# Delta-rule attention and a gated feed-forward on one core: who makes the exponent words of the weights

## The chip, the core and the metric

The kernel runs on one NeuronCore of a Trainium2 chip. The core has a matrix engine (TensorE, PE in the profile, with its weight loads shown as PEld), a vector engine (VectorE, DVE), an activation engine (ScalarE, ACT), a general engine (GpSimd, POOL) and a queue engine that issues most of the transfers (SyncE, SP). Each engine takes its instructions strictly in the order in which they were written down for it and waits on semaphores for the others. The metric is the device time of one execution in microseconds (us).

## The reference, cut to what matters

Two blocks follow one another. The first is a delta-rule attention over 4 batches, 8 heads, 768 steps and 48 dimensions; the second is a feed-forward with 384 inputs, 2048 hidden units and a sigmoid-weighted activation.

```python
k_n = k / (norm(k) + 1e-6)
for t in range(S):                                    # attention, state 48 x 48 per head
    y[:, :, t] = q_t @ state
    state = state + beta_t * outer(k_t, v_t - state^T k_t)
x = y as (3072 tokens, 384)
h = x @ w_in                                          # 384 x 2048
out = (h / (1 + exp(-1.702 * h))) @ w_out             # 2048 x 384
```

`w_in` and `w_out` arrive in a 64-bit format (they are numpy products with a float64 scale; the kernel asserts that they are not fp32). [...] In the 64-bit word the upper 32 bits hold a sign, 11 bits of exponent and 20 bits of fraction; the lower 32 bits hold the rest of the fraction. The conversion makes a word whose exponent field is the 64-bit one less 896, clamped at zero ("the exponent word"), gives it the sign, builds the fraction as a number between 1 and 2, and multiplies the two.

## The kernel before, in words

The 768 steps are cut into 6 chunks of 128. A chunk of one batch is a unit, 24 units in all. In a unit the keys are normalized, turned, multiplied with themselves on TensorE (`gram`), and the diagonal blocks of 32 x 32 are inverted by VectorE in a long run of small multiplications and sums (`invert`, lines 543 to 628). With the inverses the unit's values are solved block by block (`solve`, `below`, `rest`): TensorE multiplies, ScalarE copies the result to `VU`, VectorE subtracts. Then come the outputs (`psY`, later `four`), copied by ScalarE to `xT`, the input of the feed-forward. `hidden` multiplies `w_in` with `xT` (`ph`), ScalarE evicts each pair of results through the activation to `gT` (or `TW`), and `both_written`, `written` and `seven` multiply `gT` with `w_out` (`po`). `ph` and `po` share two PSUM buffers (tag "moe").

The first 175 us are a prologue with its own order, written by hand. Every operation made through `vec`, `act`, `pe`, `pool` and `sync` is pinned to the program's order. In between stands background work, handed out by `fill(us)` (line 322): it pulls steps from the generator `background()` and subtracts the cost that each step yields until the budget is used up. The costs are the numbers in the `yield` lines, not measured times. The background is: the nine pieces of `w_in`, then the inversion of units 4 to 7 (`invert(1)`), then the fourteen pieces of `w_out`. A piece of `w_in` has 128 x 768 elements (two halves of each of the quarters 0, 1 and 3) or 128 x 512 (three thirds of quarter 2, called `thirds`, their words lying in `gT` buffers). A piece of `w_out` has 128 x 384 elements, two of them (named 4 and 6, each for two of the sixteen row blocks) 128 x 768. The order of `w_out` is 0, 1, 2, 3, 4 with 5, 6 with 7, 8, 13, 9, 10, 12, 11, 14, 15.

One piece (`conversion`, line 224) takes five VectorE operations and one on ScalarE, with `lo` and `hi` the lower and upper words at a stride of 8 bytes and `p` the destination seen as integers:

1. VectorE masks the exponent bits of `hi` into `p` ("the mask", cost 0.75).
2. ScalarE takes `p` times 8 plus `low`, clamped at zero ("low", cost 0).
3. VectorE joins the sign of `hi` to `p` ("the join", cost 0.95).
4. VectorE turns `hi` into 1.fraction as integers, in place (0.7).
5. VectorE adds the scaled `lo` (0.95).
6. VectorE multiplies with the destination (0.95).

`conversions` (line 275) is a pipeline of depth two: the mask and ScalarE's operation of the next piece are written down between steps 4 and 5 of this one, so a ScalarE result has two VectorE operations to arrive in. When a piece is done, `fetches` starts the transfer of a later one into the space that came free, on SP's queue.

Beside this, `prepare_early` (line 1366) prepares units 8 to 11 while the feed-forward of the first four units runs: `normalize_mixed` (line 348) squares the keys on ScalarE, sums them on VectorE (`ssq`), takes the power on GpSimd (`rn`), two small operations on VectorE, and scales the keys by eight small ScalarE operations (`KN`). TensorE's `turn` (`psT`) of that unit waits for these. It stands in TensorE's order between groups of `ph`. In the same way ScalarE's evictions of `ph` stand in ScalarE's order around the eight operations and around step 2 of the conversions.

Of the kernel before, what the change touches and what calls it, by code (L numbers as in the profile page):

```python
# [8 lines left out]
F32 = mybir.dt.float32  # L9
I32 = mybir.dt.int32  # L10
U32 = mybir.dt.uint32
AX = mybir.AxisListType
ALU = mybir.AluOpType
ACT = mybir.ActivationFunctionType
# [4 lines left out]
def kernel(  # L19
# [47 lines left out]
    cpool = ctx.enter_context(tc.tile_pool(name="const", bufs=1))  # L67
# [66 lines left out]
    vec, act, pe, pool = Engine(nc.vector), Engine(nc.scalar), Engine(nc.tensor), Engine(nc.gpsimd)  # L134
# [28 lines left out]

    low = cpool.tile([128, 1], F32, name="low")
    pool.memset(low, -896.0 * (1 << 23))
    raws = w_out.rearrange("p f d -> p (f d)").bitcast(I32)
    assert moe_w_in.dtype != F32 and moe_w_out.dtype == moe_w_in.dtype

# [38 lines left out]
    places, slots = {}, {}  # L207
# [13 lines left out]
        places[f] = as_raw(words, (1, DM))  # L221
        sync(out=as_rows(places[f])[:, 0], in_=moe_w_out[f * 128 : (f + 1) * 128, :])

    def conversion(dst, raw, shape):

        lo, hi = raw[:, :, :, 0], raw[:, :, :, 1]  # L230
        ts, stt = vec.tensor_scalar, vec.scalar_tensor_tensor
        AND, OR = ALU.bitwise_and, ALU.bitwise_or
        E1 = 1 << 20
        p = dst.bitcast(I32)
        ts(p, hi, 0x7FF * E1, None, op0=AND)
        yield 0.75
        act.activation(p, p, ACT.Relu, scale=8.0, bias=low)
        yield 0.0
        stt(out=p, in0=hi, scalar=-(1 << 31), in1=p, op0=AND, op1=OR)
        yield 0.95  # L240
        ts(hi, hi, E1 - 1, E1, op0=AND, op1=OR)
        yield 0.7
        f = lo.bitcast(F32)
        stt(out=f, in0=lo.bitcast(U32), scalar=2.0**-32, in1=hi, op0=ALU.mult, op1=ALU.add)
        yield 0.95
        stt(out=dst, in0=f, scalar=2.0**-20, in1=dst, op0=ALU.mult, op1=ALU.mult)
        yield 0.95

    def pieces():

        for i in range(4):
            if i == 2:
                for j in range(KC):
                    dst = w_in[:, j : j + 1, i * NQ : (i + 1) * NQ]
                    yield dst, thirds[j], (1, NQ), ("in", -j)
                continue
            for e in range(2):
                at = i * NQ + e * NPC
                raw = quarter(i)[:, :, e * NPC : (e + 1) * NPC, :]
                yield w_in[:, :, at : at + NPC], raw, (KC, NPC), ("in", 2 * i + e)  # L260
        i = 0
        while i < FC:
            f = order[i]
            if f in (4, 6):
                at = inside[f] * DM
                raw = as_raw(raws[:, at : at + 4 * DM], (2, DM))
                yield w_out[:, f : f + 2, :], raw, (2, DM), ("out", f)
                i += 2
            else:
                yield w_out[:, f : f + 1, :], None, (1, DM), ("out", f)  # L270
                i += 1
# [3 lines left out]
    def conversions():  # L275

        whole = list(pieces())

        def begin(i):
            dst, raw, shape, name = whole[i]  # L280
            ops = conversion(dst, places[name[1]] if raw is None else raw, shape)
            return ops, next(ops)

        after, cost = begin(0)
        next(after)
        yield cost
        for i in range(len(whole)):
            ops = after
            yield next(ops)
            yield next(ops)  # L290
            if i + 1 < len(whole):
                after, cost = begin(i + 1)
                yield cost
                next(after)
            yield next(ops)
            cost = next(ops)
            done.add(whole[i][3])
            fetches.pop(whole[i][3], lambda: None)()
            yield cost
# [11 lines left out]
    def background():  # L311

        converting = conversions()
        while ("in", 7) not in done:
            yield next(converting)
        yield from invert(1)
        done.add("inverse")
        yield from converting
# [13 lines left out]
    def normalize(n):  # L332
# [5 lines left out]
        ssq = wk.tile([128, H], F32, tag="ssq", name="ssq", bufs=4)  # L338
        vec.tensor_reduce(ssq, ksq, axis=AX.X, op=ALU.add)
        rn = wk.tile([128, H], F32, tag="rn", name="rn", bufs=4)  # L340
# [7 lines left out]
    def normalize_mixed(n):  # L348
# [4 lines left out]
        ssq = wk.tile([128, H], F32, tag="ssq", name="ssq", bufs=4)  # L353
        vec.tensor_reduce(ssq, ksq, axis=AX.X, op=ALU.add)
        rn = wk.tile([128, H], F32, tag="rn", name="rn", bufs=4)
# [8 lines left out]
    def normalize_first():  # L364
# [5 lines left out]
        for b in range(B):  # L370
            act.activation(sq[:, b % 2], KN[b][:, :, 0:D], ACT.Square)
            vec.tensor_reduce(s[:, b], sq[:, b % 2], axis=AX.X, op=add)
        roots(x, y, t, s)
# [4 lines left out]
    def roots(x, y, t, s):  # L378

        tt, ts, stt = vec.tensor_tensor, vec.tensor_scalar, vec.scalar_tensor_tensor  # L380
        mult, add = ALU.mult, ALU.add
        ts(x, s, 1e-30, None, op0=ALU.max)
        ts(y.bitcast(I32), x.bitcast(I32), -0.5, float(0x5F3759DF), op0=mult, op1=add)
        for k in range(3):
            if k == 2:
                warm(NR, vec.memset)
            stt(out=t, in0=y, scalar=-0.5, in1=y, op0=mult, op1=mult)
            tt(t, t, x, op=mult)
            stt(out=y, in0=t, scalar=1.5, in1=y, op0=add, op1=mult)
        tt(s, s, y, op=mult)  # L390
        ts(s, s, 1e-6, None, op0=add)
        vec.reciprocal(s, s)
# [10 lines left out]
    def roots_second(areas):  # L403

        z, r = (TW[:, a : a + B * H].rearrange("p (b h) -> p b h", b=B) for a in (1792, 1856))
        for o in range(2):
            vec.tensor_reduce(z[:, 2 * o : 2 * o + 2], areas[o], axis=AX.X, op=ALU.add)
        pool.tensor_tensor(r, z, half[:, 0:1].broadcast_to([128, B, H]), op=ALU.pow)
# [134 lines left out]
    def invert(c, b0=0, nb=B):  # L543
# [10 lines left out]
        def dots(o, a, b, ny, nx, nk, negate):  # L554

            P = wk.tile([128, ny, nx, nk], F32, tag="P", name="P", bufs=1)[part]
            tt(P, a, b, op=ALU.mult)
            red(o, P, axis=AX.X, op=ALU.add, negate=negate)

# [9 lines left out]
        def diag(t, off, dims):  # L569
            return bass.AP(t.tensor, t.offset + off, [t.ap[0], [step, 2]] + dims)  # L570

        for i in range(1, HS):
# [4 lines left out]
            )  # L577
            red(diag(Yf, i, [[BS, i]]), P, axis=AX.X, op=ALU.add, negate=True)
            yield 0.35 + i * i / 240
# [652 lines left out]
    for blk in range(NB):  # L1232
# [3 lines left out]
        out=YB, in_=YB, compare_op=ALU.not_equal, fill=1.0, base=0,  # L1236
# [37 lines left out]
    for at in range(B):  # L1274
        for u in range(2):
            for half_ in range(2):
                lane = at * BS + u * 2 + half_
                other_queue(
                    out=bL[lane : (at + 1) * BS : NB],
# [165 lines left out]
```

## Time and profile before

| what | value |
|---|---|
| median of 3 runs (lowest, highest) | 721.5 us (720.91, 723.11) |
| profiled execution: its time, its span | 722.29 us, 720.6 us |
| busy: PE, DVE, ACT, POOL | 675.7, 467.4, 232.3, 251.4 us |
| mean granted clock of TensorE | 0.973 |

The span is the time from the first to the last instruction of the profiled execution. Busy times are sums over the span; an engine that is busy most of the time in one stage can be idle in the next, so the stages are read one by one. In the lists of groups and of single instructions, `out<-in` are the program's names with buffer numbers left out; `128x384` is partitions by elements; nearly all operations show line 122, the line of the helper that records them, so they are told apart by names and shapes. A matrix product of fp32 operands leaves two records. A wait is written as "engine tile <- what released it: total us, times, longest us".

### The profile page before, as it was taken

To read this page: it belongs to the slowest core of one execution; us is meant where nothing else is said; L and a number is where in the kernel's file an instruction comes from. 1 tells how busy PE (TensorE), PEld (TensorE's weight loads), DVE (VectorE), ACT (ScalarE), POOL (GpSimd) and SP (SyncE) were. 2 spreads that over 40 slices of the span, in tenths; PEclk is the share of its full clock that TensorE was granted. 3 is DMA by queue.
4 is the path that set the end of the run, shared out by engine and by line. 5 is a ranking of instruction groups with operands and counts; after the bars stand their busy time and mean duration, and the time that the engine had idled before them with its cause. 6 is when DMAs were issued, how large, how long until landed. Compare 5 with 4: busy or idle time off the path is not lost.

```text
span 720.6 us, 20434 instructions
## 1 busy us (share of the span) xinstructions
PE 675.7 (94%) x8779; PEld 583.0 (81%) x8779; DVE 467.4 (65%) x880; ACT 232.3 (32%) x553; POOL 251.4 (35%) x258
## 2 busy tenths in 40 slices
PE   9288898996999999999999999999999999999997
PEld 7166767863668888998988988988988988989997
DVE  4899999798465398497597696795793892110000
ACT  3362533561233313313323333233323223122020
POOL 6084001240237641652642733622522403304032
PEclk9678999998999999999999999999999999999999
DMA  8895854631223213214114124213122111000100
GB/s 175 142 186 110 209 108 82 144 100 45 56 51 65 51 32 83 43 37 93 28 36 93 27 48 82 45 43 63 34 52 56 32 25 31 8 23 2 28 0 23
DMA packets 129179, 46.66 MB, mean 65 GB/s; under 512 B 118848, under 2 KB 123584, under 8 KB 129088
## 3 DMA queue, kind: packets, MB, share of 16 engines
q1 hardware_dynamic: 125664, 40.94, 27.7%
q0 software_dynamic: 2240, 4.02, 2.6%
q8 instruction: 69, 1.13, 0.7%
q10 hardware_dynamic: 1184, 0.39, 0.2%
q14 instruction: 22, 0.18, 0.1%
HBM read 33.13 MB, written 11.01 MB: 61 GB/s over the span
## 4 chain that ended last, share of the span: by engine, by line
PE 54%; DVE 32%; DMA 5%; issue 4%; ACT 3%; SPq 2%; DVEq 0%; POOL 0%; ACTq 0%; POOLq 0%
PE ph L122 25%; PE po L122 17%; DVE P L122 12%; DVE YB L122 6%; PE four L122 4%; DVE w_out L122 4%; DVE NT L122 3%; DVE VU L122 3%; DMA NT<-Nd 2%; PE psT L122 2%; PE ps_warm L122 2%; PE psU L122 2%; DMA Nd<-G 2%; PE psR L122 1%; DVE w_in L122 1%
## 5 line engine op out<-in xcount | busy, mean ns | idle before, releaser
L122 PE MATMUL ph<-xT,w_in 128*128 128x256 f32 x1152 | 259.6, 383 | 2.0 <-ACT gT L122 2.0
L122 PEld LDWEIGHTS ph<-xT,w_in 128*128 128x128 f32 x1152 | 216.5, 191 | 33.2 <-ACT gT L122 2.4
L122 PE MATMUL po<-w_out,gT 128*128 128x192 f32 (+1 forms) x720 | 138.9, 348 | 5.5 <-DVE o L122 5.1
L971 POOL TENSOR_TENSOR gT<-gT 128x512 f32<-128x512 f32 x80 | 104.5, 1316 | 103.9 <-ACT gT L122 68.5
L122 PEld LDWEIGHTS po<-w_out,gT 128*128 128x128 f32 x720 | 118.9, 191 | 18.2 <-issue 8.6
L122 DVE TENSOR_TENSOR P<-NT,YB 64x2 f32<-64x2 f32 (+9 forms) x200 | 124.3, 622 | 5.8
L122 ACT ACTIVATE gT<-ph 128x512 f32<-128x512 f32 x90 | 53.6, 597 | 147.0 <-PE ph L122 145.9
L122 DVE TENSOR_REDUCE YB<-P 64x2 f32<-64x2 f32 (+9 forms) x200 | 81.7, 409 | 6.9
L122 PE MATMUL po<-TW,gT 128*128 128x192 f32 x480 | 81.8, 328 | 0.0
L122 PEld LDWEIGHTS po<-TW,gT 128*128 128x128 f32 x480 | 78.0, 190 | 0.7
L122 ACT COPY VU<-psU 32x384 f32<-32x384 f32 x96 | 45.0, 469 | 58.8 <-PE psU L122 43.9
L122 DVE TENSOR_TENSOR o<-o,po 128x192 f32<-128x192 f32 x40 | 13.8, 346 | 73.8 <-PE po L122 44.5
L122 DVE TENSOR_TENSOR VU<-VU,psR 32x384 f32<-32x384 f32 (+1 forms) x56 | 31.0, 554 | 41.9 <-PE psR L122 40.6
L839 POOL TENSOR_SCALAR_AFFINE_SELECT M<-M 64x512 f32<-64x512 f32 x40 | 29.3, 732 | 82.6 <-ACT M L122 78.8
L122 DVE TENSOR_TENSOR VU<-VU,four 128x384 f32<-128x384 f32 x19 | 10.5, 551 | 52.6 <-issue 38.7
L106 POOL DMA_DIRECT2D KN<-in_k_dram x24 | 17.1, 712 | 68.9 <-PE four L122 68.9
L122 PEld LDWEIGHTS psU<-VU,XB 32*32 32x32 f32 x1536 | 27.2, 105 | 15.9 <-DVE VU L122 7.1
L122 DVE TENSOR_TENSOR NT<-NT,bL 64x1024 f32<-64x1024 f32 (+1 forms) x9 | 11.0, 1219 | 44.2 <-DMA NT<-Nd 44.2
L341 POOL TENSOR_TENSOR rn<-ssq,half 128x8 f32<-128x8 f32 x12 | 21.8, 1819 | 45.3 <-DVE ssq L122 45.3
L122 ACT COPY xT<-four 128x256 f32<-128x256 f32 (+1 forms) x40 | 13.2, 329 | 75.7 <-DVE ST L122 73.3
L122 ACT COPY M<-four 128x512 f32<-128x512 f32 x19 | 11.1, 585 | 81.2 <-DVE VU L122 71.9
L122 PE MATMUL psU<-VU,XB 32*32 32x48 f32 x1536 | 32.1, 203 | 5.2 <-DVE VU L122 3.9
(123 smaller groups left out, 777.8 us busy)
## 6 DMA issues: line engine op xcount, KB each, us to landing
QP<-in_q_dram SPq DMA_DIRECT2D x40, 96.0 KB, 2.8
VU<-in_v_dram SPq DMA_DIRECT2D x40, 96.0 KB, 3.6
out_dram<-o SPq DMA_DIRECT2D x40, 96.0 KB, 2.2
raw<-in_moe_w_out_dram SPq DMA_DIRECT2D x9, 384.0 KB, 4.1
NT<-Nd SPq DMA_DIRECT2D x24, 128.0 KB, 2.6
XB<-Yd SPq DMA_DIRECT2D x24, 128.0 KB, 2.7
Yd<-NT SPq DMA_DIRECT2D x22, 128.0 KB, 2.1
Nd<-G SPq DMA_DIRECT2D x86, 32.0 KB, 1.7
```

The source lines that it names most:

```text
L106: dma(out=place(dst, n)[rows, :, 0:D], in_=src[b, :, t, :].rearrange("h p d -> p h d"),)
L122: return lambda *a, **kw: tc.keep_in_program_order(op(*a, **kw))
L341: nc.gpsimd.tensor_tensor(rn, ssq, half, op=ALU.pow)
L839: nc.gpsimd.affine_select(out=M, in_=M, compare_op=ALU.is_gt, fill=0.0, base=0, pattern=[[0, H], [1, CH]], channel_multiplier=-1,)
L971: (engine or nc.gpsimd).tensor_tensor(o, a, b, op=op)
```

## The change

For the pieces of `w_in` from the third on and for every other piece of `w_out` (by the piece's number in the whole list of 23: the even ones from 10 on, that is 1, 3, 6 with 7, 13, 10, 11 and 15) step 1 is no longer done by VectorE. ScalarE does three operations in place of one: the absolute value of `hi` read as fp32 ("Abs"), then the upper 16 bits of that, divided by 16 and rounded down by means of a bias of -15/32 ("floor"), which is the exponent field as a small integer, and then this times 2^23 plus `low`, clamped at zero ("low", as before but with another scale). The other pieces, 9 of 23, keep the mask. The pipeline hands out the three ScalarE operations of the next piece between the steps of this one. A piece without a mask costs the budget of `fill` 0.75 less. A constant tile `floor` is set once by GpSimd.

```diff
+    floor = cpool.tile([128, 1], F32, name="floor")
+    pool.memset(floor, -15.0 / 32)
...
-    def conversion(dst, raw, shape):
+    def conversion(dst, raw, shape, masked):
...
-        ts(p, hi, 0x7FF * E1, None, op0=AND)
-        yield 0.75
-        act.activation(p, p, ACT.Relu, scale=8.0, bias=low)
-        yield 0.0
+        if masked:
+            ts(p, hi, 0x7FF * E1, None, op0=AND)
+            yield 0.75
+            yield 0.0
+            act.activation(p, p, ACT.Relu, scale=8.0, bias=low)
+            yield 0.0
+        for _ in range(not masked):
+            act.activation(dst, hi.bitcast(F32), ACT.Abs)
+            yield 0.0
+            top = dst.bitcast(U16).rearrange("p j (n o) -> p j n o", o=2)[:, :, :, 1]
+            act.activation(p, top, ACT.Relu, scale=1.0 / 16, bias=floor)
+            yield 0.0
+            act.activation(p, p, ACT.Relu, scale=float(1 << 23), bias=low)
+            yield 0.0
...
         def begin(i):
             dst, raw, shape, name = whole[i]
-            ops = conversion(dst, places[name[1]] if raw is None else raw, shape)
-            return ops, next(ops)
-
-        after, cost = begin(0)
-        next(after)
-        yield cost
+            return conversion(dst, places[name[1]] if raw is None else raw, shape, i < 2 or name[0] == "out" and i % 2 == 1)
+
+        after = begin(0)
+        for _ in range(3):
+            yield next(after)
         for i in range(len(whole)):
             ops = after
+            more = i + 1 < len(whole)
             yield next(ops)
-            yield next(ops)
-            if i + 1 < len(whole):
-                after, cost = begin(i + 1)
-                yield cost
-                next(after)
-            yield next(ops)
-            cost = next(ops)
+            if more:
+                after = begin(i + 1)
+            for k in range(3):
+                if more:
+                    cost = next(after)
+                    if cost:
+                        yield cost
+                cost = next(ops)
+                if k < 2:
+                    yield cost
             done.add(whole[i][3])
             fetches.pop(whole[i][3], lambda: None)()
             yield cost
```

## The prediction

> **What bounds the kernel now.** I read the waits first, then the table by stage, then the chain and the instructions in order of time around two places.
>
> The waits of TensorE, for whole groups:
>
> ```profile
> engine line waited for: us in total, times, longest us
> PE psT L122 <- DMA QP<-in_q_dram: 14.0, 1, 14.0
> PE four L122 <- ACT QS L122: 7.0, 1, 7.0
> PE ph L122 <- ACT gT L122: 2.0, 1, 2.0
> ```
>
> Busy time by stage (the x counts are instructions):
>
> ```profile
> core 0: us, PE busy (x) PEld busy (x) DVE busy (x) ACT busy (x) POOL busy (x), PEclk, DMA share, GB/s
> 59.00:95.00 36.00, 31.12 (x769) 25.09 (x770) 34.83 (x51) 15.22 (x31) 6.91 (x5) 0.97 0.69 164
> 95.00:124.00 29.00, 27.00 (x283) 22.34 (x282) 27.30 (x60) 11.10 (x28) 2.05 (x1) 1.00 0.56 111
> 124.00:152.80 28.80, 27.18 (x224) 22.69 (x226) 23.77 (x46) 19.20 (x53) 11.01 (x8) 0.94 0.44 102
> 152.80:172.20 19.40, 12.37 (x93) 7.37 (x86) 18.71 (x40) 6.76 (x12) 1.24 (x1) 0.95 0.42 115
> 172.20:300.00 127.80, 126.23 (x1815) 100.45 (x1816) 79.02 (x147) 38.98 (x93) 54.33 (x55) 0.98 0.25 52
> ```
>
> The chain that ended last, at the two joints (start, length, what):
>
> ```profile
> 121.35 0.42 DVE YB L122
> 122.18 1.91 ACT KN L122 x8
> 124.09 0.49 ACT gT L122
> 124.62 1.68 PE ph L122 x6
> 126.31 0.85 PE psT L122 x4
> ...
> 171.10 0.61 ACT w_out L122
> 171.72 0.42 ACT QS L122
> 172.18 1.77 PE four L122 x32
> ```
>
> From 172 us on TensorE is busy 126.23 of 127.80 us and the end follows it: whatever moves its product `four` at 172.18 moves the end by as much. Before that VectorE is the fullest engine (34.83 of 36.00, 27.30 of 29.00, 18.71 of 19.40), and TensorE's two stops hang on it through ScalarE: 2.0 us at 122.6, where `gT` stands in ScalarE's order behind the eight key operations that wait for VectorE's `rn`; and 7.0 us at 165.2, where ScalarE's copy `QS<-ST` stands behind the last step 2 that waits for a mask. The stretch to watch is 124.0 to 152.8: there TensorE has 27.18 of 28.80 us and ScalarE 19.20. So VectorE's relief can be worth something only if TensorE, which is nearly full, comes no later to 165.2.
>
> **What is removed.** 14 masks. From start to next start in the order of time they take .59, .71, .44, .45, .34, .61 and .71 us in `w_in` (3.85) and six times .27 and once .68 in `w_out` (2.30): 6.15 us of VectorE. The 3.9 us that VectorE waits for ScalarE's step 2 (`w_out`, 3 waits) may go or grow.
>
> **What is added.** 28 ScalarE operations in a row of three, each waiting for the one before. No row shows an absolute value or an input of 16 bits at a stride. The nearest for Abs, which has no bias tile, are `QS<-ST` 128x384 at 538 ns and `TW<-KN` 128x384 at 523; for floor, which has one, `w_out<-w_out,low` 128x384 at 614, 128x768 at 942, and `w_in` 128x512 at 726. An operation that runs cannot cost below nothing; the low bound is 523 each, the high one, if the stride halved the rate, twice the row. VectorE's own reads of `hi` at that stride show no loss (most lines of `raw<-raw` have .36 us, those of the mask .35), so I take .53 and .62 (384), .85 and .94 (768), .64 and .73 (512), and keep the double for a rival. All told 4 x 1.79 + 3 x 1.37 + 6 x 1.15 + 1.79 = 20 us of ScalarE for 6.15 of VectorE.
>
> The Trainium skill, "ScalarE: Activation LUTs", section "Rules for kernel authors", says that maximum, addition and multiplication belong on VectorE rather than ScalarE. The rows agree: 352 against 1,150 ns for a piece of 384. Were the rule the whole of it, 20 us put in for 6.15 taken out would come out at +13.8; by the rows only what stands ahead of a waiting TensorE counts, and the sum below is made from that.
>
> **What is moved.** TensorE's order is unchanged, GpSimd sets one more tile at the start (hidden before 20 us) and does three weight differences (`TW<-w_out`) ahead of the second `rn`. On SP three recycled `raw` fetches now stand ahead of four `Nd<-G`, and one `w_out` fetch ahead of `QP`: they wait for finished pieces, but `Nd` of unit 8 is needed only at 177 us and that `QP` at 181, so I price this at nothing; a fetch that lands late would cost its lateness. VectorE and ScalarE are reordered, since `fill` counts no 0.75 for a missing mask and so reaches further down its list at every call:
>
> (a) In the block solves the later `VU` differences get more conversion and inversion ahead of them. Ahead of the last one of `VU_108`, at 102.06, now stand the inversion steps from 102.65 to 109.16, 6.51 us; 3.85 are gone: 104.7. So TensorE comes to the long run of `ph` about 2.7 us later, at 125.3 and not 122.6 where it stopped before.
>
> (b) The first `rn` (with it unit 8's keys) stood at 121.69, nine instructions before the inversion's end; now it stands behind all of it and behind two steps of piece 0:
>
> ```profile
> 118.08 0.55 DVE L122 TENSOR_REDUCE ssq<-ksq 128x8 f32<-128x384 f32 x1
> 121.69 0.16 DVE L122 TENSOR_SCALAR rn<-rn 128x8 f32<-128x8 f32 x1
> 121.88 0.20 DVE L122 RECIPROCAL rn<-rn 128x8 f32<-128x8 f32 x1
> 122.00 0.64 DVE L122 TENSOR_TENSOR P<-NT 128x512 f32<-128x512 f32 x1
> ```
>
> From 122.00 to the first step on `w_out` at 129.28 are 7.28 us, two steps of piece 0 .87: 8.15 more, less the 3.85 removed: 126.0. `ssq` moves to 123.5, and GpSimd's power after it takes 2.05 us with .6 on the way there, so `rn` can't come before 126.4.
>
> (c) Between the keys and `gT` ScalarE now also does floor and low of piece 1: 1.1 us. `gT` follows `rn` by 2.3 us before (121.69 to 124.00), now by 3.4: 129.8.
>
> (d) The first piece of quarter 3 has Abs in ScalarE's order ahead of copies. Its twelve transfers are issued until 76.5 and take 5.6 to land: 82. Abs could start at 81, and the rest of the piece follows on VectorE, where the join (83.9 by my count) would wait until 85.7. Between .7 and 1.8; I take 1.2, and 131.0 for `gT`. Before, the mask at 85.34 hid this.
>
> TensorE, itself 1.2 later by (d), arrives at 126.5 and resumes .6 after `gT` begins: 131.6, 7 us later than 124.62, having stopped 5 us and not 2.0.
>
> (e) From there to the last eviction `TW` (152.80 before, 28.8 us after the first `gT`) ScalarE was busy 19.20 us with five step 2s (3 x .62 + 2 x .95 = 3.8). Now pieces 2, 3, 4, 6, 8, 13, 9 and 10 stand there: four masked (3 x .62 + .95 = 2.8) and four in three operations (3 x 1.77 + 2.73 = 8.0), so 10.8, 7.0 more: 26.2. Of the 9.6 us idle some stays. Low bound none: 131.0 + 26.2 = 157.2, and TensorE alone gives the same: 29.04 us from 124.62 to the first `po` at 153.66, less .99 that it waits for `G` and some 1.6 by which its first `ph` run slow (12 records in 3.94 us, 2.65 later on), are 26.4. High bound all: 166.8. The waits that I find again in the new order are for `psT` 1.5, two for `ph` 1.5, `psG` .8, the second `rn` 1.3, `psQ` with its difference .7, the third `rn` .4: 6.2. I take 163.4, nearest to the row's own 9.6 less what the fuller queue covers.
>
> (f) `po` needs both shared buffers, so it starts behind that eviction; from 152.80 to 172.18 are 19.4 us, of which 7.03 the second stop. Behind that eviction ScalarE has steps 2 of 12 and 14, pieces 11 and 15, two copies to `VU` and two `QS`: 2 x .62 + 2 x 1.77 + .93 + 1.14 = 6.9, done at 170.3, and VectorE's last join follows near 172, so this stop is gone: 163.4 + 12.35 = 175.8 for `four`, against 172.18.
>
> **Sum.** +3.6 us. The profiled execution took 722.29 us, span 720.6 and 1.69 around it, .8 over the median: 725.9 for it, 725.1 against the median of 721.5. Nothing after 172 takes it back: TensorE is full there.
>
> **The rivals.**
>
> - *VectorE's relief arrives whole.* For it: VectorE is the fullest engine until 172, and both stops hang on it. The 6.15 us come off the second stop of 7.03: 715.4. It decides if TensorE is not late at the first joint; (b) speaks against it, since that is VectorE work put ahead of `rn`, not ScalarE's cost.
> - *ScalarE keeps pace.* The first joint is late, but ScalarE fills all its idle time: last eviction at 157.2, `four` at 169.6, 2.6 us less: 718.9. Its point is 159.8; beyond it the change loses. Against it: six named waits in the new order.
> - *Hidden both ways*, the delay of `ph` just fills the old stop: 721.5, from an eviction at 159.8.
> - *The strided reads run at half rate.* Abs and floor of the four pieces in (e) take 5.2 us more, floor of piece 1 .6: +9.4, 730.9. Only the missing rows speak for it.
>
> **How the numbers follow.** Forecast .52, range of its own 723 to 728.7 (by (e), bounded above by all idle time kept, +7); relief whole .12; ScalarE keeps pace .16; hidden .10; half rate .10. About 0.3%, 2.2 us, is what a measurement can tell here: 719.3 to 723.7. Faster: .12 and half of .16, .20. Same: the other half, .10, and .01 of the forecast, .19. Slower .61. The range leaves out the first rival and most of the last: 717.5 to 729.5.
>
> **What would show it.** In the new profile: VectorE's busy time down some 6 us and ScalarE's up 20, with Abs near .53 and floor near .62 for 384; the first `rn` at 126 to 128; TensorE waiting 4 to 6.5 us for `gT` and hardly for `QS`; the last `TW` at 161 to 166; `four` near 176. It is wrong if `gT` comes by 126 or if ScalarE's evictions run on without the key operations holding them; then `four` comes before 172.

## The result, and the profile after

The change made the kernel slower: 728.25 us (median of 8 runs, 725.18 to 731.48) against 721.91 us (median of 8, 720.91 to 723.11), a ratio of 1.0087 with a 95% interval of 1.0066 to 1.0108. That is 6.3 us. The profiled execution of the change took 731.48 us, the longest of its eight, with a span of 729.8; so its times below can lie up to 3 us behind those of a middle run, and the experiments are read by their medians first.

TensorE's waits, for whole groups (engine, line, what is waited for: us in total, times, longest):

```profile
engine line waited for: us in total, times, longest us
PE psT L123 <- DMA QP<-in_q_dram: 14.7, 1, 14.7
PE psU L123 <- DVE VU L123: 6.1, 6, 1.7
PE ph L123 <- ACT gT L123: 5.8, 1, 5.8
```

The first stop has grown from 2.0 to 5.8 us, the second one (`four` behind `QS`, 7.0) is gone from the list, and in the block solves `psU` waits 6.1 us for VectorE's `VU` differences, where it waited 3.9 before (also in six goes).

The table by stage, at the cuts of the profile before:

```profile
core 0: us, PE busy (x) PEld busy (x) DVE busy (x) ACT busy (x) POOL busy (x), PEclk, DMA share, GB/s
59.00:95.00 36.00, 32.08 (x641) 26.01 (x638) 29.99 (x40) 26.13 (x46) 6.51 (x5) 0.78 0.65 159
95.00:124.00 29.00, 25.31 (x387) 20.78 (x388) 27.19 (x58) 9.49 (x20) 0.00 (x0) 1.00 0.37 80
124.00:152.80 28.80, 23.04 (x126) 19.23 (x125) 21.07 (x35) 15.15 (x32) 6.11 (x5) 0.88 0.57 120
```

The first row is the one to look at. VectorE was busy 34.83 of 36.00 us there before and is busy 29.99 now: it stands idle for 6.0 us where it stood idle for 1.2. ScalarE is busy 26.13 us in place of 15.22. TensorE's granted clock in that row is 0.78, and was 0.97.

Instructions in order of time, first VectorE's around the end of the inversion, then TensorE's (start, length, what; in brackets the idle time ahead and who ended it):

```profile
110.39 0.56 DVE L123 TENSOR_TENSOR VU<-VU,psR 32x384 f32<-32x384 f32 x1
...
129.37 0.54 DVE L123 TENSOR_REDUCE ssq<-ksq 128x8 f32<-128x384 f32 x1
129.83 1.22 DVE L123 TENSOR_TENSOR NT<-YB,bL 128x1024 f32<-128x1024 f32 x1
130.96 0.56 DVE L123 SCALAR_TENSOR_TENSOR w_out<-raw,w_out 128x384 int32<-128x384 int32 x1
131.55 0.36 DVE L123 TENSOR_SCALAR raw<-raw 128x384 int32<-128x384 int32 x1
132.61 0.17 DVE L123 TENSOR_SCALAR rn<-rn 128x8 f32<-128x8 f32 x1 [0.70 <-POOL rn L123]
```

```profile
117.74 13.22 PE L123 MATMUL ph<-xT,w_in 128*128 128x256 f32 x60
136.71 2.93 PE L123 MATMUL ph<-xT,w_in 128*128 128x256 f32 x6 [5.76 <-ACT gT L123]
...
183.55 1.00 PE L123 MATMUL four<-QS,kT 48*64 48x112 f32 x32
```

So the long `ph` run begins at 117.74 (109.40 before), `rn` comes at 132.61 (121.69), TensorE goes on at 136.71 (124.62), and `four` starts at 183.55 (172.18) without a wait.

ScalarE's new operations, from its groups with shapes kept apart (between the bars: us in total and mean ns of one):

```profile
L123 ACT ACTIVATE w_in<-w_in,floor 128x768 int32<-128x768 uint16 x4 | 3.8, 938 | 0.2
L123 ACT ACTIVATE w_out<-w_out,floor 128x384 int32<-128x384 uint16 x6 | 3.7, 612 | 0.1
L123 ACT ACTIVATE w_in<-w_out 128x768 f32<-128x768 f32 x4 | 3.7, 916 | 1.0 <-issue 1.0
L123 ACT ACTIVATE w_out<-raw 128x384 f32<-128x384 f32 x4 | 2.2, 548 | 2.0 <-DMA raw<-in_moe_w_out_dram 2.0
```

Floor has the price of the prediction (.62 and .94), Abs a little more (.55 and .92 in place of .53 and .85). The strided 16-bit read costs nothing extra: the rival of half rate falls with these lines.

### The profile page after: what moved, and what is told of

Read it like the earlier page. It is cut to its first block, busy times and chain, and to the rows that moved or that the text cites. A ratio compares the mean times of both kernels' runs of the same rounds, so it can differ in the third digit from the quotient of the medians.

```text
span 729.8 us, 20464 instructions
## 1 busy us (share of the span) xinstructions
PE 683.6 (94%) x8779; PEld 588.7 (81%) x8779; DVE 461.9 (63%) x866; ACT 251.5 (34%) x581; POOL 251.5 (34%) x259
## 4 chain that ended last, share of the span: by engine, by line
PE 50%; DVE 17%; ACT 3%; DMA 3%; issue 3%; SPq 1%; DVEq 0%; ACTq 0%
PE ph L123 22%; PE po L123 18%; DVE P L123 9%; PE four L123 4%; DVE YB L123 4%; DMA NT<-Nd 2%; DVE VU L123 2%; PE psT L123 2%; PE psU L123 2%; PE psR L123 2%; DVE NT L123 1%; DMA Nd<-G 1%; SPq L551 1%; ACT KN L123 1%; ACT M L123 1%
## 5 line engine op out<-in xcount | busy, mean ns | idle before, releaser
L123 DVE TENSOR_TENSOR o<-o,po 128x192 f32<-128x192 f32 x40 | 13.8, 346 | 73.8 <-PE po L123 44.5
L123 PE MATMUL ps_warm<-ident 128*128 128x256 bf16 x235 | 36.8, 319 | 1.4 <-POOL floor L123 1.4
```

The source lines that it names most:

```text
L123: return lambda *a, **kw: tc.keep_in_program_order(op(*a, **kw))
```

## The experiments

Three places stood to be told apart: ScalarE's added 20 us, the block solves in which TensorE now loses time (step (a)), and the first `rn` behind the whole inversion (step (b)). The last two come from one thing: `fill` counts no 0.75 for a mask that is not there, and so reaches further down VectorE's list.

One difference goes with every run that is made from the change. In its pipeline a masked piece, too, is handed out otherwise than before: the mask stands before step 4 and ScalarE's step 2 between steps 5 and 6, where both stood between steps 4 and 5. No run leaves this out. In the run with `w_out` alone, counted, where all of `w_in` is masked and counted, the first joint comes 0.2 us later than before, so up to there it costs little; behind it its share is open.

The table has the ratio of each run to the kernel before, measured beside it on the same chip, and from its one profiled execution the times (us) of TensorE's long `ph` run, of `rn`, of TensorE going on behind the first stop, of `four`, and the length of the two stops.

| run | ratio (95%) | `ph` run | `rn` | goes on | `four` | stops |
|---|---|---|---|---|---|---|
| before | 1 | 109.4 | 121.7 | 124.6 | 172.2 | 2.0, 7.0 |
| the change | 1.0087 (1.0066 to 1.0108) | 117.7 | 132.6 | 136.7 | 183.6 | 5.8, none |
| whole, order kept | 1.0031 (1.0017 to 1.0044) | 109.3 | 121.6 | 124.5 | 172.7 | 2.0, 4.7 |
| order alone | 1.0106 (1.0084 to 1.0127) | 116.0 | 130.9 | 134.4 | 179.1 | 5.1, none |
| `w_in` alone | 1.0059 (1.0035 to 1.0083) | 115.8 | 130.7 | 133.7 | 179.4 | 4.6, none |
| `w_out` alone | 0.9988 (0.9974 to 1.0002) | 109.5 | 121.7 | 124.7 | 172.4 | 2.0, 3.4 |
| catch-up | 0.9975 (0.9960 to 0.9989) | 117.8 | 128.6 | 131.6 | 174.0 | 0.5, 0.2 |
| `rn` late | 1.0115 (1.0100 to 1.0129) | 110.8 | 132.2 | 136.3 | 179.9 | 12.3, none |
| more filler | 1.0077 (1.0063 to 1.0092) | 116.1 | 131.0 | 135.1 | 179.3 | 5.8, none |
| `w_out` alone, counted | 1.0056 (1.0041 to 1.0071) | 109.6 | 121.9 | 124.8 | 174.7 | 2.0, 4.7 |
| catch-up and filler | 0.9956 (0.9941 to 0.9971) | 115.0 | 125.7 | 128.7 | 171.3 | 0.5, 1.4 |
| order alone, catch-up | 1.0036 (1.0018 to 1.0054) | 117.3 | 128.1 | 131.0 | 175.0 | 0.5, 1.5 |
| `w_in` alone, catch-up | 1.0041 (1.0021 to 1.0061) | 116.4 | 127.2 | 130.1 | 177.0 | 0.5, 1.7 |
| before, filler | 1.0008 (0.9988 to 1.0028) | 110.2 | 122.5 | 125.4 | 171.3 | 2.0, 7.0 |

The profiled execution of the catch-up is the longest of its twelve (722.76 us against a median of 719.06), so its times can lie up to 3.7 us behind those of a middle run. In the run with `w_in` alone the profile puts the end of the stop down to a transfer, `XB<-Yd`, and not to `gT`; `rn` is as late there as in the other runs with the order of the change.

### Is it the order or ScalarE's work?

The change whole, with the count put back:

```diff
             act.activation(dst, hi.bitcast(F32), ACT.Abs)
-            yield 0.0
+            yield 0.75
```

> The change whole, but a piece without a mask still costs the background budget 0.75, so each call of the filling reaches exactly as far down its list as before: ScalarE's three operations stay, only the shift of the order is undone. Theory order (the loss comes from the block solves' differences and the first rn standing behind more inversion and conversion): first rn at 118 to 121 us and the first eviction behind the keys by 126 and not 136; 716 to 721 us. Theory ScalarE (the loss comes from three operations for one, ahead of the evictions): last eviction before the po products still 6 us or more later than 152.8; 726 to 729 us. Theory clock (TensorE's granted clock falls to a half in the block solves, because it waits there longer than its filler lasts): as by order if the clock in 75 to 95 us is 1.0 again; 726 or more if it still falls.

Measured: 724.35 us, between the ranges of the two theories. `rn` is back in its place, the loss is not all gone, and the granted clock from 75 to 95 us is 0.91 and not 1.0. And the reverse, all masks on VectorE and nothing new on ScalarE, but the count taken away:

```diff
-        if masked:
+        if True:
             ts(p, hi, 0x7FF * E1, None, op0=AND)
-            yield 0.75
+            yield 0.75 if counted else 0.0
...
-        for _ in range(not masked):
+        for _ in range(0):
```

`counted` is what `masked` was, so the 14 masks are made and not counted.

> All pieces keep the mask on VectorE and the single ScalarE operation, but the pieces that lost it in the change count nothing for it in the background budget: the shift of the order alone, without any ScalarE work added and without any VectorE work removed. Theory order: first rn at 130 to 134 us, 726 to 732 us. Theory ScalarE: 720 to 723 us. Theory clock: slower only if the granted clock in 75 to 95 us falls below 0.9.

Measured: 729.65 us, as much as the whole change, with none of ScalarE's 20 us; the granted clock from 75 to 95 us is 0.93 (it falls to 0.50 behind that, from 95 to 100), so the theory of the clock, which asked for less than 0.9, does not explain it. The order alone makes a loss of this size. With the order kept 0.31% of 0.87% is left. In the profiled pair 0.5 us of that is there at `four`, and 0.7 us more by the next product `four<-QS,ST`, which comes 8.9 us behind it and not 8.2, as the half clock behind `four` lasts longer; the rest was not taken apart.

The first run says a second thing. It has 14 masks less on VectorE, but `rn` and the last instruction of the inversion come where they came before (before: 121.69 and 128.14):

```profile
121.58 0.16 DVE L123 TENSOR_SCALAR rn<-rn 128x8 f32<-128x8 f32 x1
128.03 1.22 DVE L123 TENSOR_TENSOR NT<-YB,bL 128x1024 f32<-128x1024 f32 x1
```

Of 3.85 us taken off VectorE's list in `w_in`, 0.1 us arrives at the first joint. The rest turns into waits in the block solves: from 59 to 124 us VectorE waits 1.2 us for `xT`, 0.9 for ScalarE's steps on `w_in` and 0.9 for `psR`, where before the change no wait is listed at all. The traces, of one execution each, show where. VectorE's two `ST` differences, before:

```profile
83.98 0.36 DVE L122 TENSOR_TENSOR ST<-psY,ST 128x192 f32<-128x192 f32 x1
87.27 0.35 DVE L122 TENSOR_TENSOR ST<-psY,ST 128x192 f32<-128x192 f32 x1
```

With the order kept, and between them the join of the next piece:

```profile
82.10 0.36 DVE L123 TENSOR_TENSOR ST<-psY,ST 128x192 f32<-128x192 f32 x1
83.15 0.69 DVE L123 SCALAR_TENSOR_TENSOR w_in<-gT,w_in 128x512 int32<-128x512 int32 x1 [0.69 <-ACT w_in L123]
87.00 0.36 DVE L123 TENSOR_TENSOR ST<-psY,ST 128x192 f32<-128x192 f32 x1 [1.24 <-ACT xT L123]
```

So VectorE does get ahead, by 1.9 us at 82.10 (0.5 of it was there at 59 us). Then it waits for ScalarE, and by the next `VU` difference it is where it was (87.66, before 87.65). Both waits lead back to the work that ScalarE was given. The join waits for "low", the third operation in the row. `xT` is late because TensorE is. Its product `psY` waits for ScalarE's copies to `VU`, and they stand behind floor and low:

```profile
81.63 0.73 ACT L123 ACTIVATE w_in<-w_in,floor 128x512 int32<-128x512 uint16 x1
82.40 0.72 ACT L123 ACTIVATE w_in<-w_in,low 128x512 int32<-128x512 int32 x1
83.14 0.96 ACT L123 COPY VU<-psU 32x384 f32<-32x384 f32 x2
```

So `psY` waits 1.26 us (0.51 before) and then runs at half the clock, 0.50 from 83.7 to 86.5 us: its first half takes 1.97 us in place of 1.09.

### Which of the two parts?

The condition for a mask is changed, once so that only `w_in`'s pieces lose theirs, and once only `w_out`'s:

```diff
-            return conversion(..., i < 2 or name[0] == "out" and i % 2 == 1)
+            return conversion(..., i < 2 or name[0] == "out")
```

> Only the seven pieces of w_in lose the mask; all of w_out keeps it, and costs the budget as before. Theory order: the block solves and the first rn are as late as in the change (rn at 128 to 133), but the evictions behind have no added ScalarE work: 723 to 727 us. Theory ScalarE with its place in the evictions: no added work stands there, so 720 to 723 us. Theory clock: all of the loss is already here, 726 to 729 us.

```diff
-            return conversion(..., i < 2 or name[0] == "out" and i % 2 == 1)
+            return conversion(..., name[0] == "in" or i % 2 == 1)
```

> Only the seven pieces of w_out lose the mask; w_in is as before. The first rn and the block solves stand where they stood. Theory order: nothing is late at the first joint, VectorE has 2.3 us less: 718 to 722 us. Theory ScalarE: the stretch of the evictions has up to 7 us more on ScalarE, last eviction at 156 to 160 and 722 to 726 us. Theory clock: the clock does not fall, 718 to 722 us.

Measured: 726.85 us, within the ranges of the theories of the order and of the clock, and 720.59. Most of the loss lies in `w_in`'s seven pieces, whose missing counts move the block solves and `rn`. `w_out`'s seven can't be told from no change: the last `TW` comes at 156.41 in place of 152.21, and the stop at `four` shrinks from 7.0 to 3.4 us, so that `four` stays at 172.4.

Does `w_out`'s part gain if its missing masks are counted, so that VectorE's list is that of before less seven masks? The kernel is that of `w_out` alone, with the 0.75 of the first experiment:

```diff
             act.activation(dst, hi.bitcast(F32), ACT.Abs)
-            yield 0.0
+            yield 0.75
```

> Only w_out's seven pieces lose the mask, and each missing mask is counted at 0.75, so that VectorE's order is that of before less seven masks (the run without the count had ratio 0.9988). All theories: the first stop unchanged, gT at 124.0. If 2.3 us of VectorE could be had behind it, four comes by up to 2 us earlier, 719 to 720.5. If the three operations of ScalarE in a row eat it, four at 172 to 172.7 and 721 to 722.

Measured: 725.51 us, slower by 0.56%, which none of the theories expected. VectorE waits 8.2 us in three goes for ScalarE's `w_out` steps from 131 to 155 us (3.9 in three before), and `four` comes at 174.66. The uncounted order has such waits too, 9.2 us in seven goes, and pays nothing for them: its last `TW` comes later (156.41 against 155.36), but from there to `four` it takes 16.0 us, and 19.3 counted. Why was not taken apart.

### Block solves, or `rn`?

Both are late in the change. The catch-up leaves the block solves as the change has them and puts `rn` back; the other does the reverse, the count kept for `w_in` and 8.5 taken off behind the block solves, so that `rn` stands exactly where the change has it:

```diff
             yield 0.35 + i * i / 240
+            if c == 1 and i == 12:
+                for _ in range(7):
+                    yield 0.75
```

> The change whole, and its order kept in the block solves; only behind them, after the twelfth step of the inversion, seven empty steps of 0.75 are counted, so that the first rn and the keys of unit 8 stand again where they stood before the change (two inversion instructions from it), and floor and low of piece 1 stand behind gT. Theory 'rn' (the loss comes from rn standing behind the inversion): TensorE may come late out of the block solves, but the second stop (7 us before the change) takes that up; gT at about 127.5, the long ph run goes on at about 131 with no wait or a short one, the last TW at 158 to 160, four at 172 to 174, 722 to 725 us. Rival 'block solves' (TensorE's 8 us lost there are what is paid): 727 to 729, as the whole change.

```diff
             act.activation(dst, hi.bitcast(F32), ACT.Abs)
-            yield 0.0
+            yield 0.75 if counted else 0.0
...
             yield 0.35 + i * i / 240
+            if c == 1 and i == 12:
+                yield -8.5
```

Here `counted` is true for `w_in`'s pieces.

> The reverse of the former: w_in's missing masks are counted at 0.75, so the block solves have the order of before, and behind them, after the twelfth step of the inversion, 8.5 are taken off in one go, so that the first rn stands where the change has it: behind the whole inversion and two steps of piece 0. Theory 'rn': rn at 129 to 130, gT at 132 to 134, a stop of TensorE of 9 to 11 us in front of it, four at 176 to 178, 727 to 730 us. Rival 'block solves': no more than 0.5 us over the run with the whole order kept, 724 to 725.

Measured: 719.06 us, 0.25% faster than before and faster than either theory had it, and 729.77 us, no faster than the change itself. TensorE in the catch-up, and then in the run with `rn` late:

```profile
117.83 13.22 PE L123 MATMUL ph<-xT,w_in 128*128 128x256 f32 x60
131.55 1.56 PE L123 MATMUL ph<-xT,w_in 128*128 128x256 f32 x6 [0.50 <-ACT gT L123]
```

```profile
110.77 13.22 PE L123 MATMUL ph<-xT,w_in 128*128 128x256 f32 x60
136.29 2.93 PE L123 MATMUL ph<-xT,w_in 128*128 128x256 f32 x6 [12.29 <-ACT gT L123]
```

TensorE comes to the stop 7 us earlier in the second, and goes on 4.7 us later. It gains nothing from early block solves because `rn` ends the wait: at 132.2 here, at 132.6 in the change. So the late `rn` with what hangs on it, and not the 8 us that TensorE loses in the block solves, is what the change pays for; with `rn` in time those 8 us are covered by the old second stop. Two limits: both edits move all that stands behind the twelfth step of the inversion, not `rn` alone; and what the catch-up gives back depends on what else was moved, as the last of the experiments shows.

### The granted clock

The profile of the change shows half the clock in the middle of the block solves (the last three numbers of a row are PEclk, DMA share and GB/s):

```profile
75.00:80.00 5.00, 3.91 (x114) 3.18 (x116) 4.67 (x8) 2.57 (x6) 0.00 (x0) 0.79 0.84 241
80.00:85.00 5.00, 4.78 (x84) 3.57 (x80) 2.52 (x5) 3.32 (x7) 0.00 (x0) 0.50 0.91 246
85.00:90.00 5.00, 4.13 (x64) 3.93 (x64) 3.26 (x6) 4.12 (x8) 0.00 (x0) 0.68 0.54 123
```

Before, all three are 1.00. The catch-up has the half clock too (0.76 from 59 to 95 us) and is faster than before, so it can't be what the 6.3 us go for. Longer fillers on TensorE, which compute nothing that is used, test whether that costs time:

```diff
-    NW, NR, NA, NY, NU = 80, 11, 3, 38, 12
+    NW, NR, NA, NY, NU = 80, 11, 3, 38, 20
```

> The change whole, with 20 in place of 12 filler products of TensorE (13 in place of 8, 10 in place of 6) in every step of the block solves, which compute nothing that is used. Theory 'clock' (a part of the loss is that TensorE's granted clock falls to half while it waits for the VU differences, 0.50 at 80 to 85 us): granted clock 0.95 or more from 70 to 90 us, the last VU_108 difference at 107 to 109 in place of 110.4, 725 to 727 us and less spread between the runs. Rival 'order alone' (the clock falls because TensorE waits and costs nothing by itself): the fillers stand in TensorE's way, 728 to 730.

> The change whole with the catch-up behind the block solves (719.06 without more) and with the longer fillers of TensorE in the block solves (20 for 12). Theory 'clock': with rn no longer late it is the block solves themselves that set TensorE's path (it waited .5 us for gT there), so the 1.8 us that the fillers gave the last VU_108 difference pay: TensorE at the joint by 129 to 130, 717.3 to 718.5 us. Rival 'order alone': the fillers give nothing, 719 to 720.5.

> The kernel before the change with the longer fillers alone (20 for 12). Theory 'clock': its granted clock has no half-rate dip beyond 65 us, and both stops of TensorE have slack, 2.0 and 7.0 us, so nothing is gained, 721 to 722.5. Rival: the fillers by themselves make the kernel faster, 719 to 720.5, whatever the change does.

The first is the change with the fillers, the second the catch-up with them, the third the kernel before with them. Measured: 726.97, 719.10 and 723.37 us. On the change the clock is back at 1.00 in all three rows, the last `VU_108` difference comes at 108.73 in place of 110.39 and `rn` at 130.95 in place of 132.61, though the profile of the change is that of its longest run. That is what theory "clock" expected, and so is the time; but the ratios, 1.0077 and 1.0087, lie within each other's intervals. On the catch-up the ratio goes from 0.9975 to 0.9956, again with intervals that overlap, and the time, 719.10 after 719.06 us, is the rival's. On the kernel before, where all three rows are at 1.00 already, nothing is gained; its 723.37 us lie above both ranges, with an interval that takes in no change. (Its clock does fall beyond 65 us, behind the two stops, see the last section.) So a share of the half clock in the loss, 0.1 to 0.2% by the ratios, isn't settled. The catch-up with the fillers has the lowest ratio of all, 0.9956 with an interval of 0.9941 to 0.9971; it isn't told apart from the catch-up alone.

### Is the catch-up's gain the relief, or a better order?

The catch-up on the kernel with all masks on VectorE, and on the one with `w_in` alone:

> All masks on VectorE and nothing new on ScalarE, but the changed order of VectorE (none of the 14 masks counted) together with the catch-up behind the block solves. If the gain of the run with the catch-up is VectorE's relief: rn 3 to 4 us later than there, 131 to 132, a stop of 3 us or more for gT, 722 to 726 us. If it is the order that the catch-up makes and not the relief: 718.5 to 720.5.

> Only w_in's seven pieces lose the mask, with the catch-up behind the block solves; all of w_out is as before the change. If w_out's part is needed for the gain: VectorE's 2.3 us of masks stand before QS again, TensorE stops 1.5 to 3 us in front of four, 720.5 to 722.5 us. If w_in's part alone gives it: 718.5 to 720.

Measured: 724.18 and 724.59 us, both slower than before, and the second above both of its ranges. So the order that the catch-up makes is no gain by itself; it pays with ScalarE's operations in both parts. The first expectation was wrong on the place: `rn` came at 128.1, no later than with the relief, and the first stop was 0.5. What is lost shows behind the last `TW`. From its start to `four` it is 16.0 us with all masks and 17.0 with `w_out`'s, against 13.7 and 13.8 in the two catch-up runs without them. Four of `w_out`'s seven masks lie there, 1.1 us; the other 1 to 2 us were not taken apart.

This also limits what was said of `rn`. With `w_in` alone the catch-up brings `rn` from 130.7 to 127.2 and the first stop from 4.6 to 0.5 us, but the ratio goes only from 1.0059 to 1.0041, within the intervals. With all masks on VectorE it goes from 1.0106 to 1.0036, and on the whole change from 1.0087 to 0.9975.

## Why the prediction was right and wrong

The direction, the place of the loss and the range were right: slower, at the first joint, through `rn` moved behind the inversion. It came to 6.3 us and not 3.6. Of the signs, TensorE's wait for `gT` (5.8 us), the busy times (VectorE 5.5 us less, ScalarE 19.2 more) and the price of floor came as said. `rn` (132.6), the last `TW` (170.2) and `four` (183.6) came later than the ranges given for them. That the time still lies within the range, near its upper end (721.5 and 7 make 728.5, not 728.7), is in part luck: at `four` the profiled pair lies 11.4 us apart, and 2.4 us come back behind it for a reason that the prediction had ruled out. Step by step:

- **What is removed** holds the term that was wrong: "3.85 are gone", used in (a) and in (b). The 6.15 us were counted about right as work (VectorE's busy time fell from 467.4 to 461.9 us), but they were subtracted from the time of VectorE's list. The run with the order kept shows what they were worth by the first joint: 0.1 us. VectorE got up to 1.9 us ahead and gave it back in waits for ScalarE and, through ScalarE, for TensorE. I read a full engine as the bound. ScalarE's added work I priced behind the block solves, in (c) and (e), and in them only as the one wait of (d).
- **(a)** The last `VU_108` difference was to come 2.7 us later, and came 8.3 later. The 6.51 us of inversion ahead of it are right. The 3.85 did not come off, VectorE waited 5.1 us instead (3.3 for `psR`, 1.6 for the join of (d)), and the block solves began 1.1 us later in this execution. No cost of it shows: the catch-up has the same block solves and is faster than before.
- **(b)** From 121.69, 8.15 us more and 3.85 less were to give 126.0, at least 126.4. Without the 3.85 it would have been 129.8, and the run with the order alone, which has all masks and so nothing removed, measured 130.89. The change has 132.61, the slower block solves of this execution included. What sets `rn` in both is `ssq`: I put it at 123.5, and it comes at 129.37 in the change, one instruction before the end of the inversion; GpSimd's power behind it ends the wait of 0.70 us ahead of `rn`.
- **(c)** was right: `gT` follows `rn` by 3.5 us (132.61 to 136.08), 3.4 were predicted.
- **(d)** was right in kind and near in size: the join of quarter 3's first piece waits 1.61 us for ScalarE, .7 to 1.8 predicted. It is one of the waits that eat the relief, and not a term of its own.
- **(e)** had the reason only in part. From `gT` to the end of the last `TW` I priced 32.4 us, of which 26.2 were ScalarE's work; it took 34.7. The run with the order alone has 33.3 there without one new operation on ScalarE, and the two catch-up runs and the one with the order kept have 30.0 with all of them, against 28.8 before. But `w_out` alone, whose first stop is as before, has 32.9, and 31.8 counted. So what ScalarE's work costs there, 1.2 to 4.1 us, hangs on the order. The change has a longer stop ahead as well, with some 3 us of half clock behind it (see the last section); the two were not parted.
- **(f)** was right: the second stop is gone, and from the end of the last eviction (170.75) to `four` are 12.8 us, 12.35 predicted.
- **"Nothing after 172 takes it back"** was wrong by 2.4 us, in favour of the change. From one `four<-QS` to the next it takes 21.2 us before (172.18 to 193.39) and 18.8 after (183.55 to 202.39), because before the change `four` started on a clock halved by the stop. So the +11.4 at `four` of the profiled pair ends as +9.2 of span, and as +6.3 between the medians.
- **SP's order, priced at nothing:** ScalarE waits 1.95 us for a late `raw` at 178.5, but `four` starts without a wait, so the price holds here.

Of the rivals none came as put. The catch-up is 2.5 us faster than before, and its order with all masks on VectorE 2.2 us slower, so the moved work pays there; but not as 6.15 us, and not all of it need be VectorE's relief.

## What to carry to other kernels

Work taken off an engine is worth what the next joint gets of it. An engine at 97% busy need not be the bound: where engines hand small products round in a ring, ask what the engine that takes the work over does to the ring. Where a list is interleaved by counted costs, an edit that changes a cost moves everything behind it. Count the same as before, or look at which small instruction that someone waits for (here `rn`, 0.17 us) has gone behind a large one, and put it back first; only then is the edit itself measured.

## What the runs showed of the hardware

A stop of TensorE costs more than its length. The kernel before, behind its second stop of 7.0 us:

```profile
172.00:175.00 3.00, 2.82 (x34) 2.24 (x35) 1.10 (x3) 0.52 (x2) 0.00 (x0) 0.50 0.00 0
175.00:178.00 3.00, 3.00 (x7) 1.57 (x7) 2.90 (x5) 0.20 (x1) 1.54 (x2) 0.64 0.02 5
```

The change, behind its first stop of 5.8 us:

```profile
136.70:139.00 2.30, 2.29 (x5) 1.83 (x6) 2.20 (x7) 0.99 (x2) 0.43 (x1) 0.50 1.04 234
139.00:142.00 3.00, 3.00 (x11) 2.41 (x10) 2.16 (x3) 1.44 (x3) 0.82 (x1) 0.50 0.45 132
142.00:145.00 3.00, 3.00 (x42) 2.34 (x41) 0.85 (x2) 1.36 (x4) 0.00 (x0) 0.87 0.43 131
```

Behind the first the half rate lasts 4.9 us (172.2 to 177.1), behind the second 6.1 (136.7 to 142.8); half of that is lost, some 2.5 and 3 us. Behind the stop of 2.0 us of the kernel before it lasts 3.4 us, from 126.0 to 129.3. Step (e) had no term for it; it took the 1.6 us behind the shorter stop off in its low bound. With the catch-up and the fillers, where the stop is 0.5 us, the clock stays at 1.00 from 128.6 to 140.

The Trainium skill, "TensorE: Matmul & The Clock Gate", section "What's actually happening", gives the rule: half rate after an idle window of about 3.4 us, full rate after a busy one of the same length. The stops of 7.0 and 5.8 us agree with the first half of it, and the 3.4 us behind the short stop with the second. The rest does not: the half rate lasted 4.9 and 6.1 us of nearly unbroken work behind the longer stops, the stop of 2.0 us was enough to bring it on, and in the block solves of the change the clock fell at 78 us though TensorE's longest single wait since 66 us was 1.6 us. What had gone ahead there is a stretch, 74 to 76 us, with 0.52 of 2.00 us busy.

ScalarE reads 16-bit words at a stride of two at the price of a plain row: 612 ns for floor on 128x384, as for `w_out<-w_out,low` on 32-bit words (612). Abs, which reads 32-bit words at a stride of two, takes 548 ns, against 523 and 538 for the two plain rows of the prediction.
